# A first gate from token sums, attention of sequence 1 ahead of MoE 0, and loads of sequence 2 behind its stores

## The chip, the cores and the metric

The kernel runs on one core of a Trainium2 chip. A core has a matrix engine (TensorE, PE in the profile), a vector engine (VectorE, DVE), an activation engine (ScalarE, ACT), GpSimd (POOL) and SyncE (SP). Each works through its own list of instructions in order, and they wait for each other through semaphores. Sixteen DMA engines move data between the chip's main memory and the on-chip memory; in this kernel SP issues the loads of Q, K and V and the stores of the output, POOL issues the loads of the weights, and ACT loads the small gate matrix. The metric is the device time of one execution in microseconds.

## The reference, cut to what matters

For each of 8 sequences of 576 tokens there are 8 heads of width 64. Attention is the linear kind: each row of Q goes through a softmax over the head's width, each column of K through a softmax over the tokens, and then

```
kv  = k_s^T v            (64 x 64 for each head)
x   = q_s kv             (576 x 64 for each head, 576 x 512 for the sequence)
```

A mixture of experts follows, with one expert for a whole sequence:

```
pooled = mean of x over the tokens
logits = pooled @ w_gate;  e = argmax(logits);  g = softmax(logits)[e]
out    = g * (relu(x @ w1[e]) @ w2[e])       w1 512 x 1024, w2 1024 x 512
```

The expert, and so which weights are to be loaded, is known only when the attention of the sequence is done. With this draw of the inputs the experts of the sequences are 2, 3, 3, 1, 3, 3, 4 and 6: sequences 0, 1, 3, 6 and 7 load new weights, the others find theirs on the chip.

## The kernel before, in words

A sequence is worked in two halves of four heads each; half n belongs to sequence n // 2. `load` (line 114) issues the loads of Q, K and V of one half on SP, 0.59 MB each. Input buffers hold three halves. `exp_q` and `exp_k` take the exponentials on ACT and write fp16; `cast_v` casts V, on POOL or ACT; `scale_q` (140) sums the rows of Q on VectorE and multiplies by the reciprocal, on VectorE for some halves and on POOL for the others.

`kv_step` (156) computes K times V with 18 small matmuls into two PSUM banks and scales the result on VectorE into two fp16 tiles. `t_step` (174) transposes one pair of heads of Q on TensorE, nine pieces, into the spare part of the same banks, and an ACT or VectorE copy takes it out. `x_step` (187) multiplies the two: X of one pair of heads, transposed, in one PSUM tile of which there is a single one. VectorE takes it out to fp16 and sums over the tokens in the same instruction (199). These sums are `pooled`.

`gate_step` (204) multiplies `pooled` by the gate matrix (208), finds the largest logit and its index, compares the index with the experts already on the chip (`hist`, five slots), and has POOL read the index and issue the loads of W1 (255) and, in `load_w2`, of W2 (266). For sequences after the first these loads carry a condition: nothing is moved when the expert is on the chip. The loads convert the weights to fp16. `gate_exp`, `gate_split` and `gate_spread` make the gate factor and spread it over the partitions. `fetch` (297) copies the weights of a sequence from the slot where they lie to the sequence's own slot, in four VectorE pieces (306); when they were newly loaded the copy goes from the slot to itself, and it waits for the load.

`moe` (311) is a generator of 17 pieces: eight units for the hidden layer (lines 320 and 325, and a ReLU on ACT at 329), then eight half tiles and a tail for the output (339 and 354, evicted by ACT and stored by SP).

The order on every engine is written by hand. A prologue (418 to 453) does sequence 0 and part of sequence 1. Everything else has a tick, a number in a table (`at`, 371), twelve ticks for each sequence: KV of half n at its base, the transposes and X after it, the gate ten ticks after the base of the sequence, and the fetches just ahead of the MoE that uses the weights. Loads and exponentials of a half stand some ticks ahead of it. The MoE loop (454 to 460) moves the tick forward after each piece and emits all that is due, so that attention steps fall between MoE pieces. The goal of MoE b is tick 12(b+2)+10, and so the gate of sequence b+2 falls at the beginning of MoE b+1.

In the prologue, `hold_loads` (268) is a small DMA on SP that reads a corner of the first W1. SP runs in order, so the loads of halves 4, 5 and 6 behind it wait until that W1 has arrived.

Of the kernel before, what the change touches and what calls it, by code (L numbers as in the profile page):

```python
# [9 lines left out]
FP32 = mybir.dt.float32  # L10
# [9 lines left out]
def kernel(  # L20
# [52 lines left out]
    nc.gpsimd.memset(blkmask[64:128, 64:128], 1.0)  # L73
    ones_f32 = consts.tile([128, 1], FP32)
    nc.vector.memset(ones_f32, 1.0)
    ones_row = consts.tile([1, 128], FP16)
    nc.vector.memset(ones_row, 1.0)
    hist = consts.tile([1, 8], FP32)
    nc.vector.memset(hist, -1.0)
    held = consts.tile([1, 8], FP16)  # L80
    own = consts.tile([1, NS, 8], FP32)
    nc.vector.memset(own, 0.0)
    for n in range(NS):
# [90 lines left out]
    def t_step(n, g):  # L174
        eq = halves[n]["eq"]
        r = slice(64 * g, 64 * g + 64)
        tp = kv_banks(n)[g].bitcast(FP16)[:, 448:448 + S]
        for j in range(J):
            nc.tensor.transpose(out=tp[:, 64 * j:64 * j + 64], in_=eq[r, j], identity=ident[r, r])  # L179
        qt = qt_pool.tile([128, S], FP16, name="qt")  # L180
        if n < 2:
            nc.scalar.copy(qt, tp)
        else:
            nc.vector.tensor_copy(out=qt, in_=tp)  # L184
        halves[n]["qt"][g] = qt

    def x_step(n, g):
        b, i = divmod(n, 2)
        c = 2 * i + g
        if c == 0:  # L190
            xt = xt_pool.tile([128, ND, S], FP16, name="xt")
            pooled = gat_pool.tile([128, ND], FP32, name="pooled")
            seqs[b] = {"xt": xt, "pooled": pooled}
        xt, pooled = seqs[b]["xt"], seqs[b]["pooled"]
        kvs, qts = halves[n]["kv"], halves[n]["qt"]
        px = bank("x")
        nc.tensor.matmul(px[:, 0:SM], lhsT=kvs[g], rhs=qts[g][:, 0:SM], start=True, stop=True)  # L197
        nc.tensor.matmul(px[:, SM:S], lhsT=kvs[g], rhs=qts[g][:, SM:S], start=True, stop=True)  # L198
        nc.vector.tensor_tensor_reduce(  # L199
            out=xt[:, c, :], in0=px[:, 0:S], in1=ones_f32.to_broadcast([128, S]),  # L200
            scale=1.0, scalar=0.0, op0=ALU.mult, op1=ALU.add, accum_out=pooled[:, c:c + 1],
        )

    def gate_step(b):
        pooled = seqs[b]["pooled"]
        pg = bank("x")
        for c in range(ND):
            nc.tensor.matmul(  # L208
                pg[0:1, 0:E], lhsT=pooled[:, c:c + 1], rhs=wg_sb[:, c, :],
# [55 lines left out]
            cs = slice(4 * hf, 4 * hf + 4)  # L265
            nc.gpsimd.dma_start(out=w2_all[:, b % NS, cs], in_=w2_src[:, cs], **seqs[b]["kw"])

    def hold_loads():

        nc.sync.dma_start(out=held, in_=w1_all[64:65, 0, ND - 1, 0:8])  # L270

    def gate_exp(b):
        ex = gat_pool.tile([1, E], FP32, name="ex")
# [91 lines left out]

    NA = 12
    ticks = {}

    def at(t, fn, *args):
        ticks.setdefault(t, []).append((fn, args))

    for b in range(B):
        for i in range(2 if b else 0):
            n, t0 = 2 * b + i, NA * b + 5 * i
            at(t0, kv_step, n)
            for g in range(2):
                at(t0 + 1 + g, t_step, n, g)
                at(t0 + 3 + g, x_step, n, g)  # L380
        at(NA * b + 10, gate_step, b)
        late = 0 if b else 5
        at(NA * b + 11 + late, gate_exp, b)
        at(NA * b + 12 + late, gate_split, b)
        at(NA * b + 14 + late, gate_spread, b)
        if b:
            for part in range(2):
                at(NA * (b + 1) + 6 + part, fetch, b, w1_all, part)
                at(NA * (b + 1) + 8 + part, fetch, b, w2_all, part)
    at(15, load_w2, 0)  # L390
    for n in range(4, 2 * B):
        t0 = NA * (n // 2) + 5 * (n % 2)
        x = 3 if n == 4 else 0
        at(t0 - 6 + x, exp_q, n)
        at(t0 - 6 + x, cast_v, n)
        at(t0 - 5 + x, exp_k, n)
        if n + 3 < 2 * B:
            at(t0 - 5 + x, load, n + 3)
        at(t0 - 4 + (x and 2), scale_q, n, nc.gpsimd)
# [15 lines left out]
    load(2)  # L415
    with tc.manual_schedule(engines={ET.PE, ET.DVE, ET.Activation, ET.Pool, ET.SP}):

        exp_q(0)
        scale_q(0, nc.vector)
        exp_k(0)  # L420
        exp_q(1)
        cast_v(0)
        scale_q(1, nc.gpsimd)
        load(3)
        t_step(0, 0)
        t_step(0, 1)
        kv_step(0)
        exp_k(1)
        cast_v(1, True)
        x_step(0, 0)  # L430
        t_step(1, 0)
        t_step(1, 1)
        x_step(0, 1)
        kv_step(1)
        cast_v(2)
        x_step(1, 0)
        exp_q(2)
        x_step(1, 1)
        exp_k(2)
        run_ticks(11)  # L440
        hold_loads()
        load(4)
        scale_q(2, nc.vector)
        exp_q(3)
        run_ticks(13)
        exp_k(3)
        cast_v(3, True)
        load(5)
        run_ticks(15)
        scale_q(3, nc.vector)  # L450
        tick = NA + 6.0
        run_ticks(tick)
        load(6)
        for b in range(B):
            units = 17
            for m, _ in enumerate(moe(b)):
                goal = NA * (b + 2) + 10
                left = units - m
                tick = min(tick + max(0.7, (goal - tick) / left), NA * (b + 3))
                run_ticks(tick)  # L460


# [28 lines left out]
```

The softmax here doesn't subtract the row's maximum and nothing guards it: scores larger than these inputs give would overflow.

## Time and profile before

| | |
|---|---|
| median of three executions | 232.3 us (231.44 to 232.44) |
| the profiled execution | 232.45 us, of which the span of instructions is 230.8 |
| TensorE busy | 179.8 us, 78% of the span |
| VectorE, ACT, POOL busy | 113.9, 108.6, 68.7 us |
| DMA queue of SP (q1) | 37.76 MB, 50.2% of 16 engines |
| DMA queue of POOL (q0) | 10.49 MB as fp16, 27.9% of 16 engines |
| first unit of MoE 0, of MoE 1, of MoE 2 | 32.47, 74.55, 95.77 us |
| X of the sequence ahead of MoE 3 released | 125.4 us |

The span runs from the first instruction to the last; the execution has 1.65 us around it. The page's strips divide the span into 40 equal slices. The chain of waits follows the work back from the last instruction. In the timeline a line gives start, duration, engine, line of the code, operation, output and inputs, and in brackets how long the engine had been idle and what released it. Line numbers are those of the kernel before; in the changed kernel the same statements stand some lines lower.

### The profile page before, as it was taken

Reading aid. Unit: us, or ns where it says so; the run is one execution under the profiler, and the core shown is the slowest. Engines: PE = TensorE matmul, PEld = TensorE weight load, DVE = VectorE, ACT = ScalarE, POOL = GpSimd, SP = SyncE. Lnnn points to the kernel's source line nnn. Section 1 sums busy time; section 2 is a strip of 40 time slices with the busy share of each in tenths; the row PEclk is TensorE's granted clock in tenths of the full one; section 3 lists DMA queues with packets and bytes.
Section 4 is the critical chain, followed back from the end, with each engine's and each line's share of the span. In section 5 each row is a group of like instructions: output and inputs, shape, how many; then the busy total and the mean of one; then the engine's idle time right before and its main releaser. Section 6 shows DMA issues by size and latency. Waiting matters only on the chain.

```text
span 230.8 us, 4509 instructions
## 1 busy us (share of the span) xinstructions
PE 179.8 (78%) x1608; PEld 94.4 (41%) x1608; DVE 113.9 (49%) x361; ACT 108.6 (47%) x167; POOL 68.7 (30%) x88
## 2 busy tenths in 40 slices
PE   0184369539934999999902999999999998999991
PEld 0152235314412554455401554555445544545540
DVE  0747965514617457765405565775676556120200
ACT  3686005450430755475510473666457423645631
POOL 1232910386202270369000443046126700600000
PEclk9999999855995999999985799999999999999998
DMA  6996799999999883989997164780254995599145
GB/s 207 382 394 250 101 156 289 396 342 275 294 296 363 261 301 84 288 232 256 276 287 272 23 199 151 200 273 4 58 128 74 169 231 119 97 181 268 31 94 112
DMA packets 28807, 48.55 MB, mean 210 GB/s; under 512 B 3184, under 2 KB 10352, under 8 KB 28784
## 3 DMA queue, kind: packets, MB, share of 16 engines
q1 hardware_dynamic: 19472, 37.76, 50.2%
q0 software_dynamic: 8736, 10.49, 27.9%
q8 instruction: 12, 0.20, 0.3%
q10 hardware_dynamic: 576, 0.02, 0.1%
q14 instruction: 11, 0.09, 0.1%
HBM read 61.88 MB, written 9.44 MB: 309 GB/s over the span
## 4 chain that ended last, share of the span: by engine, by line
PE 52%; DMA 28%; DVE 8%; issue 5%; SPq 1%; POOL 1%; POOLq 1%; ACT 1%; DVEq 0%
DMA w_all<-in_moe_w_dram 20%; PE mm L320 19%; PE mm L339 17%; DMA v_in<-in_v_dram 8%; DVE xt L199 3%; PE mm L354 3%; PE x L197 3%; PE kv L161 3%; PE kv L179 3%; PE ht L325 2%; DVE qs L143 2%; DVE w_all L306 1%; SPq L120 1%; PE x L208 1%; POOL w_all L255 1%
## 5 line engine op out<-in xcount | busy, mean ns | idle before, releaser
L320 PE MATMUL mm<-xt,w_all 128*128 128x512 f16 x256 | 67.5, 393 | 0.0
L339 PE MATMUL mm<-w_all,hsb 128*128 128x512 f16 x256 | 63.8, 388 | 0.0
L329 ACT ACTIVATE hsb<-mm 128x512 f16<-128x512 f32 x64 | 37.3, 590 | 37.6 <-PE mm L320 37.6
L146 POOL TENSOR_TENSOR eq<-eq,qsi 128x1152 f16<-128x1152 f16 x13 | 28.8, 2217 | 66.8 <-DVE qsi L145 60.4
L346 ACT ACTIVATE osb<-mm,gate 128x512 f32<-128x512 f32 x32 | 21.9, 686 | 44.2 <-PE mm L339 32.8
L306 DVE COPY w_all<-w_all 128x2048 f16 x28 | 19.1, 682 | 33.2 <-DMA w_all<-in_moe_w_dram 31.1
L199 DVE CUSTOM_DVE_ANT_0 xt<-x,ones_f 128x576 f16<-128x576 f32 x32 | 24.2, 755 | 18.0 <-PE x L198 18.0
L339 PEld LDWEIGHTS <-hsb 128*128 128x128 f16 x256 | 22.3, 99 | 25.2 <-issue 1.6
L197 PE MATMUL x<-qt,kv 128*128 128x512 f16 x32 | 14.0, 439 | 22.9 <-DVE pooled L199 21.4
L320 PEld LDWEIGHTS <-w_all 128*128 128x128 f16 x256 | 20.6, 100 | 20.1 <-issue 4.1
L179 PE MATMUL kv<-ident,eq 64*128 64x64 f16 x270 | 13.7, 200 | 16.7 <-DVE eq L146 9.3
L255 POOL DMA_DIRECT2D w_all<-in_moe_w_dram x36 | 15.1, 426 | 34.2 <-DVE hl L282 17.5
L133 POOL CAST va<-v_in 128x1152 f16<-128x1152 f32 x14 | 16.3, 1163 | 28.1 <-DMA v_in<-in_v_dram 27.9
L143 DVE TENSOR_REDUCE qs<-eq 128x18 f32<-128x1152 f16 x16 | 21.5, 1344 | 5.4 <-ACT eq L125 5.4
L325 PEld LDWEIGHTS <-w_all 128*128 128x128 f16 x256 | 16.6, 100 | 16.0 <-issue 1.6
L184 DVE COPY qt<-kv 128x576 f16<-128x576 f16 x28 | 12.7, 455 | 16.4 <-PE kv L179 16.4
L125 ACT ACTIVATE eq<-q_in 128x1152 f16<-128x1152 f32 x16 | 18.5, 1156 | 4.5 <-DMA q_in<-in_q_dram 4.5
L179 PEld LDWEIGHTS <-eq 64*128 64x128 f16 x288 | 11.1, 102 | 22.9 <-issue 14.8
L137 ACT ACTIVATE ek<-k_in 128x1152 f16<-128x1152 f32 x16 | 18.5, 1154 | 2.2 <-DMA k_in<-in_k_dram 2.2
L325 PE MATMUL ht<-xt,w_all 128*128 128x64 f16 x256 | 18.1, 194 | 0.0
L161 PE MATMUL kv<-va,ek 64*128 64x129 f16 x270 | 12.4, 243 | 4.2 <-POOL va L133 4.2
L359 ACT ACTIVATE osb_t<-mm,gate 128x256 f32<-128x256 f32 x8 | 3.8, 473 | 23.7 <-PE mm L354 23.7
(59 smaller groups left out, 120.8 us busy)
## 6 DMA issues: line engine op xcount, KB each, us to landing
q_in<-in_q_dram SPq DMA_DIRECT2D x16, 576.0 KB, 7.3
k_in<-in_k_dram SPq DMA_DIRECT2D x16, 576.0 KB, 8.9
v_in<-in_v_dram SPq DMA_DIRECT2D x16, 576.0 KB, 10.1
w_all<-in_moe_w_dram POOLq DMA_DIRECT2D x16, 512.0 KB
out_dram<-osb SPq DMA_DIRECT2D x64, 128.0 KB, 4.8
w_all<-in_moe_w_dram POOLq DMA_DIRECT2D x28, 256.0 KB
w_all<-in_moe_w_dram POOLq DMA_DIRECT2D x8, 128.0 KB
out_dram<-osb_t SPq DMA_DIRECT2D x16, 64.0 KB, 2.3
```

What stands on the lines that cost most here:

```text
L143: nc.vector.tensor_reduce(out=qs, in_=eq, op=ALU.add, axis=AX.X)
L146: eng.tensor_tensor(out=eq, in0=eq, in1=qsi.unsqueeze(3).to_broadcast([128, J, 2, Dh]), op=ALU.mult,)
L161: nc.tensor.matmul(kps[g][:, 0:129], lhsT=ek[r, j], rhs=va[r, j], start=(j == 0), stop=(j == J - 1),)
L179: nc.tensor.transpose(out=tp[:, 64 * j:64 * j + 64], in_=eq[r, j], identity=ident[r, r])
L197: nc.tensor.matmul(px[:, 0:SM], lhsT=kvs[g], rhs=qts[g][:, 0:SM], start=True, stop=True)
L199: nc.vector.tensor_tensor_reduce(out=xt[:, c, :], in0=px[:, 0:S], in1=ones_f32.to_broadcast([128, S]), scale=1.0, scalar=0.0, op0=ALU.mult ...
L306: nc.vector.tensor_copy(out=w_all[:, b % NS, cs], in_=w_all[:, ds(seqs[b]["src"], 1), cs].rearrange("p o c f -> p (o c) f"),)
L320: nc.tensor.matmul(phm, lhsT=w1_sb[:, c, fsl], rhs=xt[:, c, 0:SM], start=(c == 0), stop=(c == ND - 1),)
L325: nc.tensor.matmul(pht[:, fc * ST:(fc + 1) * ST], lhsT=w1_sb[:, c, fsl], rhs=xt[:, c, SM:S], start=(fc == 0 and c == 0), stop=(fc == NF - ...
L329: nc.scalar.activation(out=hsb[:, fc, 0:SM], in_=phm, func=AF.Relu)
L339: nc.tensor.matmul(po, lhsT=hsb[:, fc, st * 128:st * 128 + 128], rhs=w2_sb[:, fc, :], start=(fc == 0), stop=(fc == NF - 1),)
L346: nc.scalar.mul(osb, po, gate)
```

## The change

Seven things change together.

The gate of sequence 0 no longer needs X. The sum over the tokens of X is the sum over the tokens of Q, times KV. `q_sum_step` sums Q with matmuls against a column of ones, splits each sum into two fp16 numbers, and `pool_step` multiplies them by KV. X of sequence 0 is then taken out by plain copies, by VectorE for half 0 and ACT for half 1; half 2 is taken out by ACT with the sum in the same instruction.

The attention of sequence 1 is emitted ahead of MoE 0, apart from X of half 3, which comes after the first and second unit of MoE 0. The gate of sequence 1 follows the third unit. The transposes of halves 2 and 3 are copied out by ACT.

The loads of halves 4, 5 and 6 are issued after the last store of MoE 0, and `hold_loads` goes.

The tables of ticks change: `base` says where the attention of a sequence begins, `starts` where its MoE begins. KV of half 4 now comes after the seventh unit of MoE 1. The gate of sequence 3 comes after the tenth piece of MoE 2, and the attention of half 8 and KV of half 9 follow in the same MoE.

In MoE 1 the first four pieces emit nothing else.

55 matmuls of a constant are put at the head of TensorE's list (`warm`).

The load of W2 for sequence 0 is emitted after all the prologue's attention; on POOL it stands behind the W1 loads and the cast of V of half 2, which in turn now stands behind the W1 loads.

```diff
@@ t_step
-        if n < 2:
+        if n < 4:
             nc.scalar.copy(qt, tp)
@@ x_step
-        nc.vector.tensor_tensor_reduce(
-            out=xt[:, c, :], in0=px[:, 0:S], in1=ones_f32.to_broadcast([128, S]),
-            scale=1.0, scalar=0.0, op0=ALU.mult, op1=ALU.add, accum_out=pooled[:, c:c + 1],
-        )
+        if b == 0:
+            if i:
+                nc.scalar.copy(xt[:, c, :], px[:, 0:S])
+            else:
+                nc.vector.tensor_copy(out=xt[:, c, :], in_=px[:, 0:S])
+        elif n == 2:
+            nc.scalar.activation(out=xt[:, c, :], in_=px[:, 0:S], func=AF.Copy, accum_out=pooled[:, c:c + 1])
+        else:
+            nc.vector.tensor_tensor_reduce(
...
+    def q_sum_step(n):
+        eq = halves[n]["eq"]
+        if n == 0:
+            seqs["qb"] = [bank("mm"), bank("ht")]
+            seqs["hl"] = gat_pool.tile([128, ND, 2], FP16, name="qhl")
+        for g in range(2):
+            c = 2 * n + g
+            r = slice(64 * g, 64 * g + 64)
+            qb, hl = seqs["qb"][g][:, n:n + 1], seqs["hl"]
+            for j in range(J):
+                nc.tensor.matmul(qb, lhsT=eq[r, j], rhs=ones_16[r], start=(j == 0), stop=(j == J - 1))
+            nc.vector.tensor_copy(out=hl[:, c, 0:1], in_=qb)
+            nc.vector.tensor_tensor(out=hl[:, c, 1:2], in0=qb, in1=hl[:, c, 0:1], op=ALU.subtract)
+
+    def pool_step():
+        pp = seqs["qb"][0][:, 16:16 + 2 * ND].rearrange("p (c t) -> p c t", t=2)
+        for c in range(ND):
+            nc.tensor.matmul(
+                pp[:, c], lhsT=halves[c // 2]["kv"][c % 2], rhs=seqs["hl"][:, c], start=True, stop=True
+            )
+        pooled = gat_pool.tile([128, ND], FP32, name="pooled")
+        nc.vector.tensor_reduce(out=pooled, in_=pp, op=ALU.add, axis=AX.X)
...
-    def hold_loads():
-        nc.sync.dma_start(out=held, in_=w1_all[64:65, 0, ND - 1, 0:8])
+    def warm(count):
+        pw = bank("ht")
+        for n in range(count):
+            nc.tensor.matmul(pw[:, 0:128], lhsT=ident, rhs=blkmask, start=True, stop=True)
@@ the ticks
-    NA = 12
+    base = [0, 12, 32] + [12 * b + 12 for b in range(3, B)]
+    starts = [18, 28, 48, 66] + [base[b + 1] + 10 for b in range(4, B - 1)] + [base[B - 1] + 24]
+    at(18, x_step, 3, 0)
+    at(19, x_step, 3, 1)
+    at(20, gate_step, 1)
+    at(21, gate_exp, 1)
+    at(22, gate_spread, 0)
+    at(22, gate_split, 1)
+    at(24, gate_spread, 1)
+    for b in range(2, B):
...
+        at(base[b] + 10, gate_step, b)
...
+    for b in range(1, B):
+        for part in range(2):
+            at(starts[b] - 4 + part, fetch, b, w1_all, part)
+            at(starts[b] - 2 + part, fetch, b, w2_all, part)
@@ the prologue
+        warm(55)
...
+        q_sum_step(0)
         kv_step(0)
...
+        q_sum_step(1)
+        kv_step(1)
         x_step(0, 1)
-        kv_step(1)
+        pool_step()
+        gate_step(0)
         cast_v(2)
...
-        hold_loads()
-        load(4)
...
-        load(5)
...
-        load(6)
+        kv_step(2)
...
+        t_step(2, 0)
+        t_step(2, 1)
+        gate_exp(0)
+        kv_step(3)
+        x_step(2, 0)
+        gate_split(0)
+        t_step(3, 0)
+        x_step(2, 1)
+        t_step(3, 1)
+        load_w2(0)
@@ the MoE loop
+                if b == 0:
+                    tick = min(19.0 + m, 24.5) if m < 13 else 24.0 + (m - 12)
+                elif b == 1 and m < 4:
+                    continue
+                else:
+                    tick += max(0.0, (goal - tick) / (units - m))
                 run_ticks(tick)
+            if b == 0:
+                for n in (4, 5, 6):
+                    load(n)
```

## The prediction

> **What bounds the kernel now.** I read the page's strips first, then the chain of waits, then the timeline of TensorE and VectorE around each hole. In the strips (40 slices of 5.77 us) TensorE has holes in slices 3 to 5, 7, 8, 11, 12 and 20, 21, its clock halves at three of them, and the DMA engines are full through slice 13.
>
> ```profile
> PE   0184369539934999999902999999999998999991
> PEclk9999999855995999999985799999999999999998
> DMA  6996799999999883989997164780254995599145
> ```
>
> The chain of waits (start, us, what) names what ended each hole:
>
> ```profile
> 25.03 5.19 DMA w_all<-in_moe_w_dram
> 30.24 0.78 SPq L270
> ...
> 32.53 11.23 DMA v_in<-in_v_dram
> 43.91 0.30 POOL va L133
> ...
> 49.46 21.13 DMA w_all<-in_moe_w_dram
> 70.71 0.69 DVE w_all L306
> ...
> 104.00 19.84 DMA w_all<-in_moe_w_dram
> 123.94 0.69 DVE w_all L306
> ```
>
> SP holds the loads of sequence 2 until the first W1 is in (L270), V of half 4 lands at 43.76, POOL casts it, and only then requests the weights of sequence 1, whose gate was ready at 41.7. They land at 70.7. Sequence 3 also needs a new expert; its weights come 26 us after its gate. The timeline shows how this stops TensorE (start, us, what, in brackets the idle time and its releaser):
>
> ```profile
> 72.14 0.58 PE L197 MATMUL x<-qt,kv 128*128 128x512 f16 x1 [6.73 <-DVE pooled L199]
> ...
> 97.32 0.35 PE L208 MATMUL x<-wg_sb,pooled 128*1 128x8 f32 x8 [0.39 <-DVE pooled L199]
> ...
> 123.94 0.69 DVE L306 COPY w_all<-w_all 128x2048 f16 x1 [9.37 <-DMA w_all<-in_moe_w_dram]
> ...
> 172.68 0.35 PE L208 MATMUL x<-wg_sb,pooled 128*1 128x8 f32 x8 [0.39 <-DVE pooled L199]
> ...
> 190.66 0.69 DVE L306 COPY w_all<-w_all 128x2048 f16 x1 [1.84 <-DMA w_all<-in_moe_w_dram]
> ...
> 205.90 1.42 DVE L306 COPY w_all<-w_all 128x2048 f16 x2 [5.55 <-DMA w_all<-in_moe_w_dram]
> ```
>
> The copy that waits for weights (L306) stands on VectorE ahead of the eviction of X (L199), and TensorE waits for that. The same rows price an expert load, from gate matmul (L208) to the first half of W2: 26.6 us for sequence 3, with loads beside it; 18.0 for sequence 6, with almost nothing beside it. For sequence 7 (gate 194.5) W1 took 11.4.
>
> **What the Trainium skill says.** "TensorE: Matmul & The Clock Gate", Part 1: the clock is half until a window of about 3.4 us was busy and halves again after an idle one. Agrees: clock 0.50 from 44.3 to 58.0, after idle from 42.3 to 45.1. The same part, on queue depths: ScalarE and VectorE are strict FIFO. Agrees: the L306 block above. "DMA: Bandwidth & Descriptors", section "Issuing engines are not separate DMA queues": all queues share 16 engines and interleave. Agrees with 26.6 against 18.0 us.
>
> **The change part by part.** *Warm-up:* 55 matmuls of 128 columns from 1.84 us, when the mask is ready; the trace has no such row. By the 107 ns cold that the Trainium skill's page "TensorE: Matmul & The Clock Gate", Part 1, gives for that size, an estimate is 5.9 us, ending at 7.7, before the first transpose at 9.35: taken at 0. If the clock stays full into the attention of sequence 0 it saves up to 1 us; if they ran late they would cost as much.
>
> *Gate 0 from sums:* 36 one-column matmuls, nearest row the transposes (18 in 0.90 us), so 1.8 us; the first 18 hide in the wait for V's cast (10.3 to 11.5), the others before KV of half 1. Eight tiny DVE operations at 0.17 are 1.4 us. X of half 1 leaves the gate's path (two matmul pairs and two evictions, 17.75 to 20.76). POOL reads the index at about 20 instead of 22.0, so W1 of expert 0 is in at about 28 (30.2 before). The X copies that ACT takes over (nearest row, its 512-column ReLU: 0.59, and 0.19 for an accumulator read) hide under W1's load; without it they would cost 0.8 each. The trace has no one-column sum: at the least it costs nothing (all under V's cast), at the most 3.2, and the 2 us it wins are worth nothing below.
>
> *Attention 1 first:* the V cast of half 2 now stands on POOL behind eight W1 issues (4.9 us), so it runs 25.5 to 26.7. From there: KV 1.16 cold, transposes 0.9, two ACT copies 1.2 (they free the KV banks), while VectorE first finishes KV's evictions and then 3.0 us of scaling half 3 (to about 32), transposes and X alternating with ACT evictions to 33.7. MoE 0 starts at 33.7 (32.47 before). W1's earlier arrival is worth nothing. W2 of expert 0 is issued at 26.7 on POOL, behind that cast; at 18.0-11.4=6.6 us behind W1 it is in by 36 to 40, and the first half tile needs it at 44: no cost, one for one if it came later than that.
>
> *Gate 1:* three units of 0.99 and two X of 0.57 later, plus 0.9 cold: 38.9. No load is queued on SP ahead of the MoE 0 stores, and POOL is free. W1 in at 38.9+11.4=50.3, two copies to 51.7, W2 at 38.9+18.0+1 for stores=58. The copies of W2 wait for that on VectorE; behind them stands only the row sum of Q of half 4, which comes at 60 anyway. MoE 0: 33.7+15.9 (209.92 to 225.77 is a MoE alone)+1.1 X+0.5 gates+0.9 cold=52.2. MoE 1 starts at 52.5 against 74.55: 22 us ahead, but it carries the 5.4 us of attention 2 (a MoE with one sequence takes 74.55 to 95.77=21.2) that before had already done.
>
> *Loads of sequence 2 behind the stores:* first issue at 54. In the opening of the kernel the first landed 4 us after issue and the next about 1.5 apart; with W2 still moving I add 1.5: Q 59.5, V of half 4 at 62, V of half 5 at 66.5. On ACT these exps stand between ReLUs, on POOL casts and scales follow. TensorE does seven units to 59.4 and waits for KV of half 4 at 63.2 (V plus a 1.17 cast): a new hole of 3.8 us. The rest of MoE 1 is one unit 1.0, eight half tiles 6.9, the tail 1.0 and attention with gate 5.7, 14.6 in all, and 1.2 for clock and waits: end at 79 (95.77 before).
>
> *Gate 3:* eight units 7.9, two half tiles 1.7, attention 5.0 into MoE 2: 93.6 against 97.3. The gate is thus only 3.7 us earlier, and MoE 2 now has only 7 of its 17 pieces left behind the gate; before it was the whole MoE.
>
> *Weights of sequence 3:* 18.0 alone, plus what moves beside: half 11's tail, half 12 (4.6: 1.77 MB at the 386 GB/s that the stretch from 6 to 12 us shows) and the stores of MoE 2 (before, SP's queue took 53.8% of 101 to 126, 13.5 us, beside it, and the price rose by 8.6). I take 25: first half of W2 at 118.6, the second and the two queued DVE pieces to 122. As a check, from 54 on the engines owe halves 4 to 12 (9 by 4.6=41.4), two sequences of stores (10), the tail of expert 1 (4) and expert 3 (12.4, its queue's 49.6% of 101 to 126): 54+67.8=121.8, if they never idle. W1 comes at about 108, and TensorE does the rest of MoE 2 and three units of MoE 3 cold in 108 to 119, under that wait.
>
> *From there:* resume at 122, to KV of half 10 two X, two units, a gate, two units: 5.4, so 127.4, with one unit of MoE 3 left. Before, that KV is at 132.19 with five left, so the same point is 132.19+3.94=136.1. Gain 8.7. After it both orders are the same and gates 6 and 7 keep their distance from use. Span 230.8-8.7=222.1; the profiled execution took 232.45, 1.65 around the span: 223.7, less 0.15 for the median: 223.5. Sum of the path: +22.0 at MoE 1, -5.4 attention owed, -5.3 new hole, waits and clock (MoE 1 takes 26.5 instead of 21.2), and the weights of sequence 3 take back 2.6: 8.7. I say 223.
>
> **The rivals.** *The cover holds (gain larger):* sequence 2 lands without the extra 1.5, or sequence 3's weights take nearer 20; for it: the DMA strip shows slack wherever no expert loads. TensorE's cold work after W1 then sets the resume, about 117: 218. *A longer tail:* loads beside W2 took 12.6 us for one half (issue 31.1 to 43.8); if half 4 takes that, V is at 66.6, all is 4.6 later: 228. *Slower than before:* both halves of sequence 2 take 12.6: V of half 5 at 54+25=79 instead of 66.5, ACT holds the last ReLUs of MoE 1 behind that half's exps, and gate 3 moves by the same 12: 235.5. It decides from 8.7 us later, V of half 5 after 75.2. Against it: the W2 beside which half 5 would crawl is in by 58. *The change doesn't do what it says:* gate 0's early index only moves a weight load that MoE 0 no longer waits for; true in my sum already, at 0.
>
> **How the numbers follow.** Forecast (219.5 to 227) 0.52; cover holds (214 to 219.5) 0.20, below that 0.02; longer tail (227 to 231) 0.12; no change within 0.5% (1.2 us, about what this measurement can tell) 0.04; slower 0.10. Faster is 0.86. Leaving 0.1 at each end gives 215 to 230.
>
> **What would show it.** Right: MoE 1's first unit near 52.5 and no L270; a TensorE hole released by the V cast of half 4 near 60 to 63; gate 3 near 94, the L306 wait of sequence 3 ending near 119, longer than 9.4 us; full TensorE from there. Wrong: weights of expert 1 after 55, or a clock at half through MoE 1, which alone would cost up to 12 us; or sequence 3's weights taking under 20.

## The result, and the profile after

The changed kernel takes 241.57 us, the median of four executions (239.93 to 243.1), beside 232.37 for the kernel before on the same chip. The ratio is 1.039, with a 95% interval of 1.031 to 1.048: slower, where 223 was predicted. The profiled execution took 243.1 us, with a span of 241.1. Medians are over all executions of a kernel, while the ratios leave out those that ran in a slower state, so a ratio can stand slightly beside that of two medians.

The strips of the page after (40 slices of 6.03 us, busy tenths; granted clock; DMA share):

```profile
PE   6373389999278856989354689999999999999990
PEclk9755556999869975899857599999999999999997
DMA  6997990599999989157999264784052799499244
```

Past the opening, TensorE has holes in slice 10 (60 to 66 us), in 14 and 15 (84 to 96), and above all in 19 to 22 (115 to 139), with the clock down beside each of them. From slice 24 on it is full. The DMA strip has something new ahead of that: two places with almost nothing moving, slice 6 (36 to 42 us) and slice 16 (96 to 103), not long before the last hole.

The timeline of the changed kernel around the start of MoE 2, where the largest part of the time is lost (start, us, what, in brackets the idle time and its releaser). L244 is the gate matmul, L392 the tail that ends a MoE, L344 the copy of weights, L147 the scaling of Q on GpSimd, L134 the cast of V, L180 the transposes of Q:

```profile
67.53 1.16 PE L162 MATMUL kv<-va,ek 64*128 64x129 f16 x18 [5.78 <-POOL va L134]
...
80.44 0.35 PE L244 MATMUL x<-wg_sb,pooled 128*1 128x8 f32 x8
83.39 0.05 POOL L291 DMA_DIRECT2D w_all<-in_moe_w_dram  x1 [7.89 <-DMA w_all<-in_moe_w_dram]
83.59 1.06 PE L392 MATMUL mm<-w_all,hsb 128*64 128x256 f16 x16
...
84.89 0.69 DVE L344 COPY w_all<-w_all 128x2048 f16 x1 [1.44 <-DMA w_all<-in_moe_w_dram]
85.20 0.04 POOL L302 DMA_DIRECT2D w_all<-in_moe_w_dram  x1 [0.40 <-DMA w_all<-in_moe_w_dram]
...
87.32 2.37 POOL L147 TENSOR_TENSOR eq<-eq,qsi 128x1152 f16<-128x1152 f16 x1 [0.38 <-DVE qsi L146]
88.01 3.79 DVE L344 COPY w_all<-w_all 128x2048 f16 x2
89.63 1.62 POOL L134 CAST va<-v_in 128x1152 f16<-128x1152 f32 x1
92.31 0.64 PE L180 MATMUL kv<-ident,eq 64*128 64x64 f16 x9 [2.31 <-DVE kv L170]
```

The first line is the predicted hole behind the loads of sequence 2, here 5.78 us. The others are the gate of sequence 2 and what follows from it. Its expert is on the chip, so no weights move, but the requests are still issued (83.39 and on, the six of them 0.45 us apart), the four copies from the old slot to the new one still run (84.89 to 91.80), and the first of them waits for the fourth request, that of the last part of W1 (issued at 84.76, 0.13 us before the copy). The pair at 88.01 takes 3.79 us, while the other two copies take 0.65 and 0.69; GpSimd is scaling Q and casting V beside it. TensorE meanwhile does one unit of MoE 2 and KV of half 6. The same four copies in the kernel before, in its own line numbers:

```profile
89.35 0.69 DVE L306 COPY w_all<-w_all 128x2048 f16 x1 [0.34 <-DVE kv L169]
90.58 0.68 DVE L306 COPY w_all<-w_all 128x2048 f16 x1
91.92 0.68 DVE L306 COPY w_all<-w_all 128x2048 f16 x1
...
95.94 0.65 DVE L306 COPY w_all<-w_all 128x2048 f16 x1
```

There they come 13.5 us after the gate (75.86), with most of a MoE in between; in the changed kernel the gate is 4.5 us ahead of the first copy.

The timeline after from gate 3 to the resume:

```profile
108.37 0.35 PE L244 MATMUL x<-wg_sb,pooled 128*1 128x8 f32 x8 [0.99 <-DVE pooled L209]
...
123.37 0.58 PE L198 MATMUL x<-qt,kv 128*128 128x512 f16 x1 [6.92 <-DVE pooled L209]
...
133.39 0.69 DVE L344 COPY w_all<-w_all 128x2048 f16 x1 [8.58 <-DMA w_all<-in_moe_w_dram]
134.60 0.64 PE L180 MATMUL kv<-ident,eq 64*128 64x64 f16 x9 [5.62 <-DVE kv L170]
...
145.28 0.70 PE L162 MATMUL kv<-va,ek 64*128 64x129 f16 x18
```

Gate 3, predicted at 93.6, comes at 108.4, and the first half of W2 of sequence 3 is copied 25.0 us later. TensorE stops twice for these weights, 6.92 and 5.62 us, once for each matrix. KV of half 10, the equal point of the two orders, comes at 145.28; in the kernel before the same point of the work is at 136.1, as the prediction reckons it, so 9.2 us are lost there, and the spans differ by 10.3.

### The profile page after: what moved, and what is told of

Read it like the earlier page. It is cut to its first block, busy times and chain, and to the rows that moved or that the text cites. A ratio compares the mean times of both kernels' runs of the same rounds, so it can differ in the third digit from the quotient of the medians.

```text
span 241.1 us, 4685 instructions
## 1 busy us (share of the span) xinstructions
PE 190.9 (79%) x1703; PEld 103.0 (43%) x1703; DVE 115.8 (48%) x357; ACT 113.7 (47%) x177; POOL 68.1 (28%) x88
## 4 chain that ended last, share of the span: by engine, by line
PE 31%; DVE 15%; DMA 12%; issue 3%; ACT 1%; POOLq 0%; DVEq 0%; POOL 0%; ACTq 0%
PE mm L358 13%; DMA w_all<-in_moe_w_dram 12%; PE mm L377 10%; DVE w_all L344 5%; DVE qs L144 3%; PE kv L180 2%; DVE xt L209 2%; PE ht L363 2%; PE x L198 1%; PE kv L162 1%; PE mm L392 1%; DVE qt L185 1%; DVE qsi L146 1%; DVE kv L170 0%; ACT eq L126 0%
## 5 line engine op out<-in xcount | busy, mean ns | idle before, releaser
L358 PE MATMUL mm<-xt,w_all 128*128 128x512 f16 x256 | 72.1, 412 | 2.6 <-DVE w_all L344 2.5
L377 PE MATMUL mm<-w_all,hsb 128*128 128x512 f16 x256 | 61.5, 380 | 0.0
L367 ACT ACTIVATE hsb<-mm 128x512 f16<-128x512 f32 x64 | 37.5, 592 | 44.7 <-PE mm L358 44.6
L344 DVE COPY w_all<-w_all 128x2048 f16 x28 | 24.9, 890 | 47.5 <-DMA w_all<-in_moe_w_dram 46.4
L147 POOL TENSOR_TENSOR eq<-eq,qsi 128x1152 f16<-128x1152 f16 x13 | 27.8, 2139 | 54.7 <-DVE qsi L146 54.3
L358 PEld LDWEIGHTS <-w_all 128*128 128x128 f16 x256 | 21.5, 103 | 24.9 <-issue 7.0
L291 POOL DMA_DIRECT2D w_all<-in_moe_w_dram x36 | 15.2, 427 | 57.1 <-DVE hl L320 17.4
L209 DVE CUSTOM_DVE_ANT_0 xt<-x,ones_f 128x576 f16<-128x576 f32 x26 | 19.4, 747 | 17.5 <-PE x L199 17.2
L363 PEld LDWEIGHTS <-w_all 128*128 128x128 f16 x256 | 17.5, 104 | 17.7 <-issue 4.6
L134 POOL CAST va<-v_in 128x1152 f16<-128x1152 f32 x14 | 16.8, 1203 | 27.7 <-DMA v_in<-in_v_dram 27.4
L162 PE MATMUL kv<-va,ek 64*128 64x129 f16 x270 | 13.5, 254 | 13.8 <-POOL va L134 13.3
L180 PE MATMUL kv<-ident,eq 64*128 64x64 f16 x270 | 14.3, 206 | 11.6 <-DVE kv L170 9.1
L180 PEld LDWEIGHTS <-eq 64*128 64x128 f16 x288 | 12.2, 105 | 17.8 <-issue 16.1
L162 PEld LDWEIGHTS <-ek 64*128 64x128 f16 x288 | 11.6, 113 | 18.0 <-issue 12.1
L185 DVE COPY qt<-kv 128x576 f16<-128x576 f16 x24 | 10.9, 453 | 9.8 <-PE kv L180 9.5
```

Source lines behind the costliest of these rows:

```text
L147: eng.tensor_tensor(out=eq, in0=eq, in1=qsi.unsqueeze(3).to_broadcast([128, J, 2, Dh]), op=ALU.mult,)
L162: nc.tensor.matmul(kps[g][:, 0:129], lhsT=ek[r, j], rhs=va[r, j], start=(j == 0), stop=(j == J - 1),)
L209: nc.vector.tensor_tensor_reduce(out=xt[:, c, :], in0=px[:, 0:S], in1=ones_f32.to_broadcast([128, S]), scale=1.0, scalar=0.0, op0=ALU.mult ...
L344: nc.vector.tensor_copy(out=w_all[:, b % NS, cs], in_=w_all[:, ds(seqs[b]["src"], 1), cs].rearrange("p o c f -> p (o c) f"),)
L358: nc.tensor.matmul(phm, lhsT=w1_sb[:, c, fsl], rhs=xt[:, c, 0:SM], start=(c == 0), stop=(c == ND - 1),)
L363: nc.tensor.matmul(pht[:, fc * ST:(fc + 1) * ST], lhsT=w1_sb[:, c, fsl], rhs=xt[:, c, SM:S], start=(fc == 0 and c == 0), stop=(fc == NF - ...
```

## The experiments

All kernels below are the changed kernel with the edit shown, cut with `...`; each was compared with the kernel before on the same chip. The chips differ, so where a kernel is set against the changed kernel, a difference of two medians can be off by one or two microseconds, and the one that the two ratios give is named where it differs by more than one. The point to read in each is gate 3, and the two times beside it: when MoE 1 ends, and when KV of half 10 begins (84.65, 108.4 and 145.3 in the changed kernel).

### The copies of sequence 2, and the hole ahead of it

The first kernel drops the copies of sequence 2: MoE 2 reads the weights where they lie. It leaves out the choice of the slot, which is written in and is right for this draw alone. The six requests stay.

```diff
-        w1_sb, w2_sb = w1_all[:, b % NS], w2_all[:, b % NS]
+        slot = 1 if b == 2 else b % NS
+        w1_sb, w2_sb = w1_all[:, slot], w2_all[:, slot]
...
-        for part in range(2):
+        for part in range(0 if b == 2 else 2):
```

> The changed kernel without the four copies of sequence 2's weights: MoE 2 reads the slot of sequence 1, which holds the same expert with this draw. Theory 1 (in the changed kernel these copies stand between the late gate of sequence 2 and MoE 2, and everything behind follows): the first unit of MoE 2 follows the tail of MoE 1 at once instead of 3 us later, T of half 6 comes at about 89 instead of 92.3, the half clock from 88 to 98 shortens or goes, gate 3 moves from 108.4 to 100 to 103, and the time falls by 5 to 8 us, to 233.5 to 236.5. Theory 2 (the late loads of sequence 2 alone): within 2 us of 241.6.

It took 237.0 us, ratio to before 1.014 (1.006 to 1.022). Its timeline of TensorE from the end of gate 2 to gate 3:

```profile
86.50 0.70 PE L162 MATMUL kv<-va,ek 64*128 64x129 f16 x18 [1.25 <-POOL va L134]
88.57 0.43 PE L180 MATMUL kv<-ident,eq 64*128 64x64 f16 x9 [1.37 <-POOL eq L147]
...
102.01 0.35 PE L244 MATMUL x<-wg_sb,pooled 128*1 128x8 f32 x8 [0.99 <-DVE pooled L209]
```

MoE 1 ends at 84.15, hardly earlier, but gate 3 at 102.0: 17.9 us later instead of 23.7. The clock now stays full from 70.4 to 114.7, where the changed kernel had half clock from 87.9 to 98.2. So the copies, with the clock that went with them here, are 5.8 us of MoE 2, and 4.6 us of the end (5.9 by the ratios).

The second kernel fills the hole instead: half 4 is loaded as soon as W2 of sequence 0 has landed, held by a small read of its corner, and halves 5 and 6 stay behind the stores. The third has both edits.

```diff
...
         load_w2(0)
+        nc.sync.dma_start(out=held, in_=w2_all[64:65, 0, NF - 1, 0:8])
+        load(4)
...
-                for n in (4, 5, 6):
+                for n in (5, 6):
```

> The changed kernel with the loads of half 4 issued as soon as W2 of expert 0 is in, into the stretch from about 38 to 45 us in which the DMA engines idle; halves 5 and 6 stay behind the stores of MoE 0. Theory 2 (late loads of sequence 2): the hole of 5.8 us in MoE 1 ahead of KV of half 4 and the half clock behind it go, MoE 1 ends at 77 to 79 instead of 84.65, gate 3 moves by the same 6 to 7, the time to 234 to 236. Theory 1: the hole goes but the copies of sequence 2 stay ahead of MoE 2, gate 3 gains less than 4, the time is 238 to 240.

> Both edits together. If the two causes are separate and add up: gate 3 at about 94 to 97 and the time 227 to 231, below the kernel before. If one hides the other: no better than the better of the two alone.

They took 240.08 us, ratio 1.024 (1.014 to 1.035), and 235.3 us, ratio 1.007 (1.004 to 1.011). The timeline of TensorE in the second kernel:

```profile
62.42 0.70 PE L163 MATMUL kv<-va,ek 64*128 64x129 f16 x18 [1.20 <-ACT ek L139]
67.41 0.60 PE L181 MATMUL kv<-ident,eq 64*128 64x64 f16 x18 [3.21 <-POOL eq L148]
71.95 0.70 PE L163 MATMUL kv<-va,ek 64*128 64x129 f16 x18
...
105.71 0.35 PE L245 MATMUL x<-wg_sb,pooled 128*1 128x8 f32 x8 [0.99 <-DVE pooled L210]
```

KV of half 4 comes 5.1 us earlier and its hole falls from 5.78 to 1.20, but the transposes now wait 3.21 for the scaled Q, and half 5, still behind the stores, comes only 2.6 earlier. That is what reaches the end of MoE 1 and gate 3 (2.7 earlier), and 1.5 us of the median (3.5 by the ratios). The hole was in plain sight in the strips and was not where most of the time was.

Both edits together did not reach 227 to 231. The timeline of TensorE in the third kernel (its profiled execution took 236.25 us, 1 us above the median):

```profile
85.85 0.66 PE L181 MATMUL kv<-ident,eq 64*128 64x64 f16 x9 [1.37 <-POOL eq L148]
86.44 1.89 PE L360 MATMUL mm<-xt,w_all 128*128 128x512 f16 x4
...
102.33 0.35 PE L245 MATMUL x<-wg_sb,pooled 128*1 128x8 f32 x8 [0.99 <-DVE pooled L210]
```

MoE 1 ends at 81.6, 2.5 us earlier than with the first edit alone, and MoE 2 has nearly the same waits (1.08, 1.37 and 0.99). But here the clock is half from 85.8 to 92.6, a unit takes 1.89 us instead of 1.04, and gate 3 is no earlier. So the gain of the earlier load is there, and in this execution the clock takes it back; without the copies the stretch to gate 3 is 17.9 us at full clock and 20.7 with this fall, against 23.7 with the copies.

### The early first gate, and the warm-up

The prediction held that the early gate 0 and the warm-up were worth nothing. One kernel takes both back (gate 0 from X, no sums, no warm-up, V of half 2 cast after gate 0 as in the changed kernel), another only the warm-up.

```diff
-        q_sum_step(0)
-        q_sum_step(1)
-        pool_step()
-        gate_step(0)
-        cast_v(2)
...
         x_step(1, 1)
+        gate_step(0)
+        cast_v(2)
```

> The changed kernel with the first gate from X again and without the 55 warm-up matmuls: the two parts that the prediction took at nothing. Theory (they are off the path): MoE 0 starts within 1.5 us of 35.6 and the time stays within 2 us of 241.6. Rival (the gate from sums is worth what it brings the first index forward, 2 us, or the warm-up costs what it lasts): 244 or 236.

> The changed kernel without the 55 warm-up matmuls; nothing else moves. Theory 1 (their clock is lost at 9.4 us, before most of the first attention runs): within 0.7 us of the changed kernel, 240.9-242.3. Theory 2 (they carry the first matmuls at full clock and bring gate 0 forward): gate 0 0.5 us or more later than 19.2, time 242.5-244; the 2.9 us that the first gate from X cost would then be partly theirs.

The first took 244.44 us, ratio 1.047 (1.039 to 1.055), 2.9 us more than the changed kernel (1.7 by the ratios); the second 241.29, ratio 1.036 (1.028 to 1.044), 0.3 us less, with gate 0 at 18.93. So the warm-up does nothing that can be measured here, and the early gate does 2 to 3 us of good. How, TensorE shows in the kernel without it and, in the last line, in the changed kernel:

```profile
30.78 1.16 PE L162 MATMUL kv<-va,ek 64*128 64x129 f16 x18 [8.13 <-POOL va L134]
...
27.68 1.16 PE L162 MATMUL kv<-va,ek 64*128 64x129 f16 x18 [6.17 <-POOL va L134]
```

Gate 0 comes 3.1 us later (22.29 instead of 19.19) and KV of half 2 comes 3.1 us later (30.78 instead of 27.68), because it waits for a cast that stands on GpSimd behind the eight requests of W1, which gate 0 starts. MoE 0 does not wait for its weights; it waits for that cast, so an earlier gate is passed on one for one: gate 3 is 3.0 us later (111.34).

### What the late weights are worth

The next kernel asks for the weights of sequence 3 at the start of MoE 2, with the expert's number written in. It leaves out one part of the computation: the request does not depend on gate 3.

```diff
+        if b == 3:
+            seqs[b].update(zz=zz, nmx=nmx, sidx=sidx, kw={})
+            return
...
+    def early_w3():
+        w1_src = moe_w1[1:1+1].rearrange("o (i h g e) f -> i h e (o g) f", i=2, h=2, g=2)
...
+    at(49, early_w3)
```

> The changed kernel with one thing different: the weights of sequence 3 are requested at tick 49, at the start of MoE 2 (some 85 us), for an expert number written into the kernel (the one that this draw's gate finds), so they no longer wait for gate 3. Gate 3, the loads' sizes and every other order stay. This leaves part of the computation out: the request does not depend on the gate. Theory 1 (what costs the time is that gate 3, and with it W3, comes late): the two stops of TensorE at 116.4 to 123.4 and 129.0 to 134.6 (6.92 + 5.62 = 12.5 us) and the half clock around them (10 us of matmul at half clock, 5 us) go; KV of half 10 moves from 145.3 to about 128, the time from 241.6 to 222-228. Theory 2 (the loads of halves 8 to 10 would be pushed back by the weights, since both share the DMA engines): other stops take their place, KV of half 10 not before 138, time 233-238.

It took 226.56 us, ratio 0.975 (0.969 to 0.981): inside what theory 1 expected, and below the kernel before. Its timeline of TensorE:

```profile
106.56 0.35 PE L244 MATMUL x<-wg_sb,pooled 128*1 128x8 f32 x8 [0.98 <-DVE pooled L209]
...
117.58 0.38 PE L198 MATMUL x<-qt,kv 128*128 128x512 f16 x1 [2.02 <-DVE pooled L209]
...
129.30 0.70 PE L162 MATMUL kv<-va,ek 64*128 64x129 f16 x18
```

Gate 3 is as late as in the changed kernel (less 1.8), but of the 12.5 us of stops 2.0 and a stop of 1.1 are left. The clock stays full from 95.5 us until past KV of half 10, which comes 22.7 us after gate 3 instead of 36.9.

This does not show that the rest of the changed order is a gain. The kernel before waits for the same weights (9.37 us, in the prediction's lines), and it was not run with an early request. What gate 3 is worth can be read from all the profiled executions together. From gate 3 to the end of the span the kernel before takes 133.5 us (230.8 less 97.3), the changed kernel 132.7, and the eleven other kernels of this document in which the request waits for gate 3 take 131.8 to 134.9; this kernel alone takes 118.0. So the changed kernel is slower because its gate 3 comes 11.0 us later than that of the kernel before, and because the stretch behind it is as long as it was.

### Gate 3 earlier, by order alone

Two edits of order leave nothing out. One moves the attention of sequence 3 four ticks ahead (which also brings the cast of V of half 6 ahead of the requests of gate 2), the other puts the cast of V of half 2 ahead of gate 0 on GpSimd.

```diff
-    base = [0, 12, 32] + [12 * b + 12 for b in range(3, B)]
+    base = [0, 12, 32, 44] + [12 * b + 12 for b in range(4, B)]
```

```diff
-        gate_step(0)
         cast_v(2)
+        gate_step(0)
```

> The changed kernel with the attention of sequence 3 four ticks earlier (base[3] 44 instead of 48; MoE 2 has 17 units in 18 ticks), so gate 3 stands behind some 6 units of MoE 2 instead of 10, and the V cast of half 6 ahead of gate 2 on GpSimd; nothing else moves. Theory 1 (the end follows gate 3 by a fixed stretch): gate 3 at 102-105 instead of 108.4, W2_3 copied 25 us later, time 235-238. Theory 2 (the loads of halves 6 and 7 aren't there that early, so KV of half 6 or 7 waits and stops MoE 1's tail): gate 3 at 107 or later, time 240-243.

> The changed kernel with the V cast of half 2 ahead of gate 0 on GpSimd, so ahead of the eight requests of W1_0 (issued 21.5 to 26.4) instead of behind them. Theory 1 (gate 0 sets when MoE 0 starts only because the cast stands behind its requests): KV of half 2 at 22.5-24 instead of 27.7, gate 1 at 38-40 instead of 41.1, time 1 to 3 us less: 238.5-240.5. Theory 2 (MoE 0 then waits for W1_0 instead): KV of half 2 as early, but the first unit of MoE 0 at 34.5 or later (35.6 before) and gate 1 not before 40.3, time 240.5-242.

The first took 237.96 us, ratio 1.019 (1.012 to 1.027), gate 3 at 102.2, first half of W2 copied at 128.4 (26.2 later). The second took 237.32, ratio 1.021 (1.015 to 1.027), with gate 3 at 101.8 and the copy at 127.0 (25.3 later). The timeline of TensorE in the second:

```profile
21.40 1.16 PE L162 MATMUL kv<-va,ek 64*128 64x129 f16 x18 [0.43 <-ACT ek L138]
...
34.85 0.34 PE L244 MATMUL x<-wg_sb,pooled 128*1 128x8 f32 x8
...
61.33 1.16 PE L162 MATMUL kv<-va,ek 64*128 64x129 f16 x18 [5.84 <-POOL va L134]
```

KV of half 2 comes 6.3 us earlier, which is the 6.17 us of idle time it had, and this lead stays whole through gate 1 (6.25), KV of half 4 (6.2) and gate 3 (6.6), where theory 1 expected at most 3 us: the move of one cast was worth more than I thought, since MoE 0 starts at 29.9 and finds its weights there. (The span of the profiled execution is 7.2 us shorter, the median 4.3; executions of one kernel lie 2 to 3 us apart.) The hole ahead of half 4 is as long as before, because its load stands behind the stores, and these move with MoE 0.

The next kernel joined both, in a bolder form, with the load of half 4 behind W2 of sequence 0:

```diff
-    base = [0, 12, 32] + [12 * b + 12 for b in range(3, B)]
+    base = [0, 12, 30, 43] + [12 * b + 12 for b in range(4, B)]
...
+        nc.sync.dma_start(out=held, in_=w2_all[64:65, 0, NF - 1, 0:8])
+        load(4)
...
-        gate_step(0)
         cast_v(2)
+        gate_step(0)
...
```

> The changed kernel with three moves together and nothing left out: the V cast of half 2 ahead of gate 0, half 4 loaded as soon as W2_0 has landed instead of behind the stores of MoE 0, and the attention of sequences 2 and 3 two and five ticks earlier (base 30 and 43). Theory 1 (gate 3 sets the end, and it is the order that makes it late): gate 3 at 95-100, W2_3 copied 25 us later (120-125), time 226-232, at or below the kernel before. Theory 2 (the loads of halves 5 to 7 set gate 3, whatever the order): gate 3 at 103 or later, time 235-240.

It took 244.33 us, ratio 1.048 (1.041 to 1.054), outside both, with gate 3 at 108.4. Its timeline of VectorE and TensorE:

```profile
52.37 1.42 DVE L345 COPY w_all<-w_all 128x2048 f16 x2 [12.28 <-DMA w_all<-in_moe_w_dram]
53.12 1.76 PE L359 MATMUL mm<-xt,w_all 128*128 128x512 f16 x4 [4.43 <-DVE w_all L345]
...
76.67 1.16 PE L163 MATMUL kv<-va,ek 64*128 64x129 f16 x18
```

With the earlier cast gate 1 comes at 35.0, and half 4 is issued at 37.5, in the same moment as the weights of sequence 1. These then take 17.4 us to their first copy instead of 11.6, and MoE 1 begins with a stop of 4.43. The idle DMA stretch into which the load was put is there only as long as gate 1 is late; with the earlier cast it is taken. How much of the late gate 3 is this load, and how much the two bolder bases, was not taken apart.

Without that load, and with the two edits as they were alone:

> The changed kernel with two moves of order and nothing left out: the V cast of half 2 ahead of gate 0 on GpSimd, and the attention of sequence 3 four ticks earlier (base[3] 44). Alone they gave 237.3 and 238.0 against 241.6. Theory 1 (both act through the time of gate 3, one on all before it and one on the units of MoE 2 ahead of it, so they add): gate 3 at 95.5-97, KV of half 10 at 134-136, time 232-235, level with the kernel before. Theory 2 (with the start 6 us earlier and the loads of halves 5 to 7 where they were, the loads set gate 3): gate 3 at 99 or later, time 236-238.

It took 232.8 us, ratio 1.002 (1.000 to 1.005): level with the kernel before. Gate 3 is at 96.3, where 108.4 less 6.2 less 6.6 would be 95.6. The two gains add.

Two more kernels move the load of half 4 on top of this: first to the landing of W1 of sequence 1, then, with half 5 beside it, to the first copy of that W1.

```diff
+    def load_4():
+        nc.sync.dma_start(out=held, in_=w1_all[64:65, 1, ND - 1, 0:8])
+        load(4)
+    at(22, load_4)
...
```

```diff
+    def load_4():
+        nc.sync.dma_start(out=held, in_=w1_all[64:65, 1, 0, 0:8])
+        load(4)
+        load(5)
+    at(24, load_4)
...
```

> The last kernel with one more move: half 4 is loaded when W1_1 has landed (some 46 us) instead of behind the stores of MoE 0 (51), nothing left out. Theory 1 (the 5.8 us stop of TensorE ahead of KV of half 4 is the late load, and there is nothing else behind it): KV of half 4 at 57-58 instead of 61.3, gate 3 1 to 3 us earlier than without this move, time 230-233.5, below the kernel before by up to 1%. Theory 2 (the load only takes DMA time from W2_1, whose copies then stop VectorE for longer, and half 5 takes the stop over, as when half 4 was loaded behind W2_0): gate 3 within 0.7 us of the kernel without it, or later, time 233-237.

> The kernel with the two moves of order (V cast of half 2 ahead of gate 0, attention of sequence 3 four ticks earlier) and the loads of halves 4 and 5 ahead of the stores of MoE 0, held until the first half of W1_1 has been copied by VectorE (47.5 us) instead of until it has landed, so that no copy has to wait for the small read that holds them (in the run that held half 4 on the landing of W1_1 the second copy stood 4.0 us behind that read). Nothing is left out. Theory 1 (that read, and half 5 coming after the stores, ate what the earlier half 4 gave): KV of half 4 at 58-59, of half 5 at 64-66, gate 3 at 93-95 against 96.3, time 229-231.5, below the kernel before by 0.3 to 1.3%. Theory 2 (the loads now take DMA time from W2_1, whose landing then holds MoE 1's second half): W2_1 copied at 59 or later instead of 55, gate 3 at 96 or later, time 232-234.

The first took 232.08 us, ratio 1.001 (0.998 to 1.004), with gate 3 at 97.4, 1.1 later. On VectorE one line shows why:

```profile
51.89 0.69 DVE L345 COPY w_all<-w_all 128x2048 f16 x1 [4.04 <-DMA held<-w_all]
```

The copy of the second half of W1 overwrites what the small holding read has to read first, and waits 4.04 us for it; MoE 1 waits for the copy. The second kernel avoids that, and took 231.92 us, ratio 0.997 (0.994 to 1.000). It is 0.3% below the kernel before at the middle of its interval, less than counts as a difference here, and between the ranges of the two theories. Its timeline:

```profile
57.99 0.70 PE L163 MATMUL kv<-va,ek 64*128 64x129 f16 x18 [2.62 <-POOL va L135]
63.92 0.70 PE L163 MATMUL kv<-va,ek 64*128 64x129 f16 x18
...
72.44 0.35 PE L245 MATMUL x<-wg_sb,pooled 128*1 128x8 f32 x8 [2.65 <-DVE pooled L210]
...
73.61 2.12 POOL L148 TENSOR_TENSOR eq<-eq,qsi 128x1152 f16<-128x1152 f16 x1
73.70 2.04 DVE L263 SCALAR_TENSOR_TENSOR score<-same,own 1x8 f32<-1x8 f32 x1
...
83.56 2.34 DVE L345 COPY w_all<-w_all 128x2048 f16 x1
...
95.84 0.35 PE L245 MATMUL x<-wg_sb,pooled 128*1 128x8 f32 x8
```

Halves 4 and 5 come as expected, and gate 2 is 2.7 us earlier than in the kernel it builds on (75.1). By gate 3 only 0.4 of that is left. An operation of the gate on eight numbers takes 2.04 us, 0.15 otherwise (76.76 in the kernel it builds on), because the scaling of Q had started on GpSimd 0.09 us before it, and both end at 75.7. The requests and copies of sequence 2 follow from there. The first copy starts at 79.17, against 79.81.

## Why the prediction was wrong, point by point

*The step that failed.* It is "Gate 3: eight units 7.9, two half tiles 1.7, attention 5.0 into MoE 2". It gave 14.6 us from the end of MoE 1 to gate 3; this stretch took 23.7. The step counts what TensorE does and leaves out what VectorE must do before TensorE may start: sequence 2 needs no new weights, so I gave its weights no time, although its four copies and six requests are in the code. Before, they hid behind most of a MoE. The changed order left two half tiles and the tail between gate 2 and MoE 2, and that cover was gone. The first experiment prices the copies at 5.8 of the 9.1 us missed, clock included; the third kernel, where the clock fell without them, at 3.0. What remains in the first, 3.3, is near the three waits its timeline still shows (1.25, 1.37 and 0.99, together 3.6): the V cast of half 6 stands on GpSimd behind the requests, its scaled Q behind that, and the gate behind an eviction. That these waits are the rest is read from the lines; no kernel was run without them.

*What it cost.* A late gate 3 is a late request. "I take 25" for the weights was right: 25.0 us, and 25.3 to 26.2 in the kernels with an earlier gate, though 15 us later than foreseen and so beside other transfers. The chain of error in the span is then: 5.7 us up to the end of MoE 1 (84.65 against 79), 9.1 in MoE 2, less 2.2 from gate 3 to the resume (26.2 against 28.4), 5.3 more from the resume to KV of half 10 (10.7 against 5.4), and 1.1 after it: 19.0, which is 241.1 less 222.1. The last three terms together are a second miss: the forecast needs 128.5 us from gate 3 to the end (222.1 less 93.6), and no kernel whose request waits for gate 3 came under 131.8.

*The resume.* "Three units of MoE 3 cold under that wait" failed too. Only one ran before the stop at 129: VectorE works in order, so the results of KV of half 9 (its matmuls end at 126.95) stood behind the copy that waited for W2 (133.39) and came at 134.00, and with them the transposes that are the next item of TensorE. The two units left over, the transposes of half 9 and the half clock to 139 account for about the 5.3 us.

*Gate 0 from sums and Attention 1 first.* "W1's earlier arrival is worth nothing" was right about the weights and wrong about the gate. I had written down that the cast now stands behind eight W1 requests and taken 33.7 for MoE 0's start from it, but not asked what these requests wait for. The experiments give 2 to 3 us for the early gate, and 4.3 for taking the cast out of its way. MoE 0 began at 35.16 instead of 33.7.

*Warm-up.* Zero, as predicted (241.29 without it). The 55 matmuls took 5.17 us, where the estimate was 5.9.

*Gate 1.* Predicted 38.9 (its own terms add to 38.7, and those of MoE 0's end to 52.1 instead of 52.2), came at 41.1, with the 1.5 us of MoE 0's start in it; W1 was copied at 53.0, 11.9 after the gate, 11.4 plus 0.5.

*Loads of sequence 2 behind the stores.* The hole is where it was predicted, released by the V cast of half 4, 5.78 us instead of 3.8. The first load left at 57.0 instead of 54, and the cast began 9.3 us after that, where 8 was taken (the prediction's steps of 4, 1.5 and twice about 1.5 make 8.5). MoE 1 takes 29.9 us instead of 26.5: 2.0 from the hole and the rest beside a half clock from 64.0 to 70.9. That the mechanism holds and a fix is worth only 1.5 to 3.5 us was not foreseen: half 5 and the scaling of Q stand right behind.

*The rivals.* The slower one named a late half 5 that pushes gate 3 back by 12 us. Gate 3 did go back by 14.8, and 8.7 was where it turns slower, so the place was right and the cause was not: V of half 5 was cast at 70.8, ahead of the 75.2 from which it was to decide. I gave slower a chance of 0.10, since I had only looked for loads that come late and not for engine work that loses its cover.

*The clock.* The prediction read the half clock at 44.3 in the kernel before as agreeing with an idle window of about 3.4 us. TensorE had then been idle for 2.1 us, and for 2.9 in all (42.25 to 45.12), which is less; what the traces show instead stands in the last section.

*From there.* Right: TensorE is full from KV of half 10 on and both orders take the same time but for 1.1 us. Two copies in that stretch take 2.30 us where before all took 0.65 to 0.69; whether they are the 1.1 was not tried.

## What to carry to other kernels

When an order is changed, list for each stage not only what its matrix engine does but every copy, cast and request that must be done before it, on each in-order queue, and ask what covered each of them before. A stage that loads nothing is not a stage that waits for nothing. And when the end hangs on one request that depends on data, price an edit by how far it moves that request: here what came behind gate 3 took 131.8 to 134.9 us in every order, and filling the most visible hole, 5.78 us long, moved gate 3 by 2.7.

## What the runs showed of the hardware

*Requests that move nothing cost time.* Six conditional loads whose condition is false take 0.45 us each on GpSimd, 2.7 in all, and a copy on VectorE still waits for them: the first copy of sequence 2 comes after an idle 1.44 us, and in six kernels it starts 0.13 or 0.14 us after the fourth request.

*VectorE and GpSimd lock each other out.* The Trainium skill, "SBUF — State Buffer", section "SBUF: two separate sides", says that the two share a port pair as an exclusive lock: a VectorE operation in a two-port mode, or with two inputs in SBUF beside a GpSimd operation that reads SBUF, is fully blocked while GpSimd holds it. The runs agree: a copy of 0.65 to 0.69 us takes 2.30 to 2.34 when a GpSimd scaling (2.12) has started first, and an operation on eight numbers with two inputs took 2.04 instead of 0.15. What is lost is about what the GpSimd operation has left to run, 1.6 to 1.9 us in these cases, for the large copy and the tiny operation alike. In the group of the page after, the mean of 28 copies is 890 ns (682 in the kernel before):

```profile
L344 DVE COPY w_all<-w_all 128x2048 f16 x28 | 24.9, 890 | 47.5 <-DMA w_all<-in_moe_w_dram 46.4
```

*A partly busy window lost the clock.* The warm-up gave full clock from 6.0 to 9.4 us, and then it was half until 40.1. (The column shows 1.00 ahead of the first recorded change too; that the clock rose at 6.0 shows in the pace, 34 of these matmuls in 3.40 us before it and 18 in 1.06 after it.) The windows of the changed kernel in steps of 3.4 us (start and end, length, busy time of PE, PEld, DVE, ACT and POOL, granted clock, DMA share, GB/s):

```profile
2.60:6.00 3.40, 3.40 (x34) 3.40 (x33) 0.00 (x0) 2.34 (x2) 0.00 (x0) 1.00 0.99 334
6.00:9.40 3.40, 1.13 (x21) 0.98 (x20) 2.98 (x3) 1.76 (x3) 0.00 (x0) 1.00 1.02 376
9.40:12.80 3.40, 2.05 (x54) 1.92 (x53) 2.02 (x6) 2.61 (x4) 2.06 (x2) 0.50 1.05 402
```

The Trainium skill, "TensorE: Matmul & The Clock Gate", Part 1, has the clock fall after an idle window of about 3.4 us. Here it fell after a window in which TensorE was busy for 1.13 of 3.40 us, and it did not come back after one with 2.05 of 3.40 (small matmuls, one third of them with a single column). The length of the steps agrees: all stretches of clock in this trace are near multiples of 3.4 us. Cut into such steps, the first 149 us of this trace show the clock fall five times, each time after a step with TensorE busy for 0.1 to 1.2 us, and keep it after every step with 2.4 us or more; what lies between is not shown. Warming up ahead of small, scattered matmuls is for nothing here, which the run without it confirms.
